# Scores of a unit and head: one matmul with 128 queries on tiles of 64 rows and 128 columns, in place of two with 64 queries on quarter tiles

## Chip, core and metric

The kernel runs on one core of a Trainium2 chip. The metric is the device time of one execution in microseconds (us); before the change the median of three runs is 1308.91 us. The engines are called as the profile calls them: PE (TensorE matmul), PEld (its weight loads, which lie beside the matmuls), DVE (VectorE), ACT (ScalarE), POOL (GpSimd) and SP (the engine that issues most DMAs).

## The reference

Attention over 8 batches of 8 heads, with 576 rows of 64 numbers each, in which only scores close to the row's maximum count, then a feed-forward layer with a squared ReLU on the 4608 x 512 result.

```python
scores = scale * np.matmul(q, k.transpose(0, 1, 3, 2))
thresh = np.max(scores, axis=-1, keepdims=True) - tau
scores = np.where(scores >= thresh, scores, -1000000000.0)
scores = scores - np.max(scores, axis=-1, keepdims=True)
attn = np.exp(scores)
attn = attn / (np.sum(attn, axis=-1, keepdims=True) + 1e-09)
return np.matmul(attn, v).astype(np.float32)
# (B,H,S,D) -> (B*S, H*D), then
h = np.maximum(x @ w_in, 0.0)          # 512 -> 2048
return (h * h @ w_out).astype(np.float32)
```

All matmuls are in float32. The trace shows each of them as two MATMUL records with a LDWEIGHTS each, called its two passes here.

## The kernel before

**Two stages.** The attention fills the first 512 us; the feed-forward layer (lines L825 and L960, each a product of 2 x 2 blocks with seven multiplications, nested twice) fills the rest and is not touched.

**Units.** Heads are taken in pairs, 32 in all: the 64 numbers of the first head lie on partitions 0 to 63, those of the second on 64 to 127. A pair's 576 queries are four units of 128 rows and a rest of 64; the rests of two pairs make one joint unit. So there are 144 units, 128 full and 16 joint. Keys stand as 512 (main) and 64 (rest).

**Periods.** The work is written out by hand, period by period, two units A and B to a period. In period p the scores of A = 2p and B = 2p + 1 are made, the weights of the pair of units before are masked, and the values of the pair before that are summed. Two lists give the order in which a period's steps are issued. CONVERTING is used for the first half of the attention, while POOL, DVE and ACT also convert the feed-forward weights from float64; PLAIN for the rest:

```python
PLAIN = """
    SA c3 T topA0 over U eU s1 SB topA1 powA1 leastA topB0 powB0 c1 s2 PV c4 V fetch
    inv powA0 c5 topB1 powB1 eT maskA1 x xm W eV maskA0 leastB c2 c6 eW maskB0
    maskB1
""".split()
CONVERTING = """
    fetch SA U eU T SB topA0 s1 c1 topA1 topB0 c3 V PV leastA over powA0 topB1
    powA1 powB0 c4 eT inv x maskA1 maskA0 W leastB maskB0 c5 eV c2 powB1 c6 eW maskB1 xm
""".split()
```

Every engine works through its own steps in this order and waits on semaphores for the others. The steps, with their lines in the profile:

- SA (L434, PE): A's scores with the 512 main keys, one result for each head (banks 0 and 5 of the PSUM tile `sc`), then the rest keys of A and of B (64 columns each, in banks 1 and 4). SB (L434): B's main scores, banks 2 and 3.
- T (L398, PE): transposes of a later pair's queries (8) or keys (10) into banks 1 and 4; eT (L403 and L411, ACT) takes them to SBUF, where L403 scales the queries. About every ninth period has no T.
- U, V, W (L380, PE): transposes of softmax weights; with W come the row factors (L515, PE), called "ones" below. eU, eV, eW (L523, ACT) take them to SBUF.
- PV (L532, PE): weights times values, into banks 0 and 5; x (L644 on DVE in PLAIN, L642 on ACT in CONVERTING) takes them out.
- topA0, topA1, topB0, topB1 (L452, DVE): copies a unit's scores of one head to SBUF and reduces each row. pow (L462, ACT): the exponential. mask (L467, DVE): threshold and row sum. Small steps: least (L459, POOL), over (L474, POOL), inv (L477, DVE). s1 and s2 (L122 and L125, POOL): sums of feed-forward weights.

**Tiles of the array.** The profile prints the part of the array that a matmul uses, rows by columns: `64*64` is a quarter tile, `64*128` half of the rows with all columns. Scores, ones and PV use `64*64`, the transposes T, U, V, W `64*128`. The two heads lie on different rows. A score matmul of a full unit has half of its queries, c = 0 or 1, as weights and puts them on one half of the columns, so that a unit's main scores are four matmuls on the four quarters.

**Where the halves come from.** A transpose takes 64 rows at a time. The two halves r of the queries go to two PSUM banks, and `then` in `turn` takes each half, 256 columns for four units, to its own half of `qT`.

Of the kernel before, what the change touches and what calls it, by code (L numbers as in the profile page):

```python
# [48 lines left out]
def kernel(  # L49
# [25 lines left out]
    nc = tc.nc  # L75
    B, H, S, D = q.shape
    P = 128
# [3 lines left out]
    FULL = S // P  # L81
# [190 lines left out]
    loaded, loaded_v, turned, weights = {}, {}, {}, {}  # L272
    CH = NB + FULL
    HALF = P // 2
# [57 lines left out]
    def places(i):  # L332
        if i not in turned:
            turned[i] = (
                sb.tile([P, MAIN], FP32, tag="qT", bufs=Q_RING, name="qT"),
                sb.tile([P, S], FP32, tag="kT", bufs=K_RING, name="kT"),
                sb.tile([P, REST], FP32, tag="qR", bufs=K_RING, name="qR"),
            )
        return turned[i]
# [3 lines left out]
    def ask_ahead(i, which):  # L343

        while asked[which] < min(len(pairs) - 1, i + (2 if i else 1)):
            asked[which] += 1
            (load_k if which else load_q)(asked[which])
# [7 lines left out]
    def touch(what, made, at, size, key=0):  # L355

        if at is None:
            return
        on = range(at // BANK, (at + size - 1) // BANK + 1)
        met = {made.ins.engine}  # L360
        for kind, other, others, its in reversed(touched):
            e = other.ins.engine
            if e == made.ins.engine:
                continue
            if on[-1] < others[0] or others[-1] < on[0]:
                if any({what, kind} == {x, y} and any((key - its) % n == 0 for n in rings) for x, y, rings in MEET):
                    continue
                tc.declare_no_dep(made.ins, other.ins, reason="other banks")
            elif e not in met:
                met.add(e)  # L370
                tc.add_manual_dep(made.ins, other.ins.name, behind, reason="same bank")
        touched.append((what, made, on, key))
        while len(touched) > 300:
            touched.popleft()
# [12 lines left out]
    def joined(to):  # L387

        return to.rearrange("p (t r q) -> p r t q", r=2, q=HALF)

    def turn(i, which, spots, other=None):

        nat, to = loaded.pop((i, which)), places(i)
        of = [nat[:, t, :] for t in range(FULL)] + ([loaded.pop((i, 2))] if which else [])
        for t, x in enumerate(of):
            for r, (spot, at) in enumerate(spots):
                rows = ds(r * HALF, HALF)
                made = nc.tensor.transpose(spot[:, ts(t, HALF)], x[rows, :], ident[rows, rows])  # L398
                touch("turns", made, at, BANK)
        half = FULL * HALF  # L400

        def scaled(to, spot):
            touch("turned", nc.scalar.activation(out=to, in_=spot[0], func=AF.Identity, scale=qscale[:, :]), spot[1], BANK, i)  # L403

        def then():
            part = lambda r, x, n: (spots[r][0][:, ds(x, n)], spots[r][1])
            if which:
                for r, n in ((0, half), (1, half + REST)):
                    spot = part(r, 0, n)
                    copy_by = other if r and other else nc.scalar.copy  # L410
                    touch("turned", copy_by(to[1][:, ds(r * half, n)], spot[0]), spot[1], BANK, i)  # L411
                scaled(to[2], part(0, half, REST))
                ask_ahead(i, 1)
            else:
                for r in range(2):
                    scaled(to[0][:, ds(r * half, half)], part(r, 0, half))
                ask_ahead(i, 0)

        return then
# [3 lines left out]
    def scores(n, rest):  # L423

        of, t = units[n]
        at_k, count = (MAIN, REST) if rest else (0, MAIN)
        for j in range(2):
            first = n % 2 != j
            to = (3 * j + 1) * BANK + first * (BANK - REST) if rest else (3 * j + 2 * first) * BANK
            for c in range(2):  # L430
                rows, at = ds(j * D, D), ds(c * HALF, HALF)
                qT, kT, qR = turned[of[c]]
                lhs = qT[rows, ds((c * FULL + t) * HALF, HALF)] if t < FULL else qR[rows, :]
                made = nc.tensor.matmul(  # L434
                    sc[at, ds(to, count)], lhs, kT[rows, ds(at_k, count)], start=True, stop=True
                )
                touch("scores", made, to, count, of[c])
# [170 lines left out]
    def period(p):  # L608
# [51 lines left out]
        def scored_a():  # L660
            if has(A):
                scores(A, False)
                scores(A, True)
                scores(B_, True)
                softmax(A)
# [336 lines left out]
    with tc.manual_schedule():  # L1002
        with ExitStack() as stack:
            sc = stack.enter_context(tc.tile_pool(name="sc", bufs=1, space=PSUM)).tile([P, 6 * BANK], FP32, name="sc")
# [219 lines left out]
```

## Time and profile before

| | |
|---|---|
| time, three runs | 1307.8, 1308.91, 1309.66 us (median 1308.91) |
| profiled execution | 1308.12 us, of which its span 1306.3 us |
| busy in the span | PE 1284.5 us (98%), PEld 1159.8, DVE 1010.8 (77%), ACT 845.7, POOL 916.4 |
| L434 matmuls (scores) | 2304 records, the first at 7.6 us, the last at 498.9 us |
| granted TensorE clock | 0.998 of full speed |

The 1.8 us between span and time lie outside the profiled instructions. Matmul records overlap: a matmul's recorded duration holds its way through the array, so the distance from the start of one group to the start of the next is what a group costs PE, and that is how the rows of the timeline are read here. "x16" counts records, two for each matmul.

### The profile page before, as it was taken

Reading aid. Unit: us, or ns where it says so; the run is one execution under the profiler, and the core shown is the slowest. Engines: PE = TensorE matmul, PEld = TensorE weight load, DVE = VectorE, ACT = ScalarE, POOL = GpSimd, SP = SyncE. Lnnn points to the kernel's source line nnn. Section 1 sums busy time; section 2 is a strip of 40 time slices with the busy share of each in tenths; the row PEclk is TensorE's granted clock in tenths of the full one; section 3 lists DMA queues with packets and bytes.
Section 4 is the critical chain, followed back from the end, with each engine's and each line's share of the span. In section 5 each row is a group of like instructions: output and inputs, shape, how many; then the busy total and the mean of one; then the engine's idle time right before and its main releaser. Section 6 shows DMA issues by size and latency. Waiting matters only on the chain.

```text
span 1306.3 us, 47872 instructions
## 1 busy us (share of the span) xinstructions
PE 1284.5 (98%) x19483; PEld 1159.8 (89%) x19483; DVE 1010.8 (77%) x2431; ACT 845.7 (65%) x1498; POOL 916.4 (70%) x1023
## 2 busy tenths in 40 slices
PE   8999999999999999999999999999999999999998
PEld 5777777677777777999999999999999999999998
DVE  5999999999999996877787778777646654665463
ACT  5999999888898985657665766675523432433240
POOL 2777778755555320978897789768777777777775
PEclk9999999999999999999999999999999999999999
DMA  6565666544333313466556665569645234522511
GB/s 153 145 160 140 169 182 188 147 103 104 89 78 79 79 41 80 133 200 218 182 181 194 203 208 164 180 247 393 245 158 162 63 105 158 162 68 96 162 34 33
DMA packets 247035, 192.12 MB, mean 147 GB/s; under 512 B 97184, under 2 KB 195488, under 8 KB 246816
## 3 DMA queue, kind: packets, MB, share of 16 engines
q1 hardware_dynamic: 245504, 188.66, 48.5%
q8 instruction: 153, 2.51, 0.8%
q14 instruction: 66, 0.54, 0.2%
q10 hardware_dynamic: 1312, 0.41, 0.1%
HBM read 116.65 MB, written 72.35 MB: 145 GB/s over the span
## 4 chain that ended last, share of the span: by engine, by line
PE 87%; ACT 5%; DMA 3%; DVE 3%; issue 1%; POOL 1%; SPq 0%; ACTq 0%; DVEq 0%; POOLq 0%
PE po L960 29%; PE ph L825 28%; PE sc L532 11%; PE sc L434 10%; PE pt L380 5%; DVE arena L452 3%; ACT arena L462 2%; PE sc L515 2%; DMA wall<-w 2%; PE sc L398 2%; ACT arena L523 1%; PE sc L380 1%; DMA g<-arena 1%; ACT arena L403 0%; ACT c L771 0%
## 5 line engine op out<-in xcount | busy, mean ns | idle before, releaser
L125 POOL TENSOR_TENSOR arena<-arena 128x512 f32<-128x512 f32 (+1 forms) x314 | 378.1, 1223 | 129.1 <-DVE arena L125 115.1
L960 PE MATMUL po<-wall,arena 128*128 128x128 f32 x3528 | 394.7, 275 | 1.4 <-ACT arena L737 1.4
L960 PEld LDWEIGHTS po<-wall,arena 128*128 128x128 f32 x3528 | 394.3, 192 | 1.8 <-ACT arena L737 1.8
L825 PE MATMUL ph<-arena,wall 128*128 128x128 f32 x3528 | 394.2, 275 | 0.7 <-DVE arena L644 0.7
L825 PEld LDWEIGHTS ph<-arena,wall 128*128 128x128 f32 x3528 | 394.0, 192 | 0.8 <-issue 0.8
L125 DVE TENSOR_TENSOR arena<-ph,arena 128x512 f32<-128x512 f32 x378 | 256.3, 688 | 86.3 <-PE ph L825 63.2
L122 POOL TENSOR_TENSOR arena<-arena 128x128 f32<-128x128 f32 (+2 forms) x314 | 255.4, 814 | 53.8 <-DMA arena<-w 37.6
L125 DVE TENSOR_TENSOR arena<-po,arena 128x128 f32<-128x128 f32 x378 | 108.4, 290 | 168.6 <-PE po L960 164.5
L467 DVE SCALAR_TENSOR_TENSOR arena<-arena 128x576 f32<-128x576 f32 x288 | 237.4, 860 | 1.3 <-POOL arena L459 0.8
L452 DVE TENSOR_SCALAR_CACHE_REDUCE arena<-sc 128x576 f32<-128x576 f32 x288 | 205.0, 747 | 14.6 <-ACT arena L523 4.8
L462 ACT ACTIVATE arena<-arena 128x576 f32<-128x576 f32 x288 | 208.1, 773 | 11.8 <-DVE arena L452 8.5
L771 ACT COPY c<-arena 128x512 f32<-128x512 f32 (+1 forms) x303 | 173.5, 579 | 49.6 <-DVE arena L122 41.7
L532 PEld LDWEIGHTS sc<-arena 64*64 64x64 f32 x5760 | 159.2, 133 | 36.7 <-DVE arena L452 20.2
L532 PE MATMUL sc<-arena 64*64 64x128 f32 (+1 forms) x5760 | 180.8, 262 | 2.7 <-DVE arena L452 1.3
L434 PE MATMUL sc<-arena 64*64 64x64 f32 (+1 forms) x2304 | 176.9, 414 | 6.2 <-ACT arena L403 4.2
L122 DVE TENSOR_TENSOR arena<-arena,c 128x512 f32<-128x512 f32 (+1 forms) x267 | 174.9, 663 | 5.5 <-ACT c L771 4.0
L523 ACT COPY arena<-pt 128x1024 f32<-128x1024 f32 x144 | 146.4, 1017 | 30.5 <-PE pt L380 29.4
L737 ACT COPY arena<-po 128x128 f32<-128x128 f32 x63 | 16.6, 264 | 186.7 <-PE po L960 184.0
L380 PEld LDWEIGHTS pt<-ident,arena 64*128 64x128 f32 x2304 | 83.4, 139 | 39.4 <-ACT arena L523 30.1
L737 ACT COPY arena<-ph 128x512 f32<-128x512 f32 x63 | 36.6, 581 | 123.1 <-PE ph L825 122.5
L434 PEld LDWEIGHTS sc<-arena 64*64 64x64 f32 x2304 | 74.3, 134 | 45.1 <-ACT arena L403 15.1
L380 PE MATMUL pt<-ident,arena 64*128 64x64 f32 x2304 | 102.2, 228 | 2.3 <-ACT arena L523 2.3
(50 smaller groups left out, 922.2 us busy)
## 6 DMA issues: line engine op xcount, KB each, us to landing
g<-arena SPq DMA_DIRECT2D x144, 256.0 KB, 2.6
arena<-g SPq DMA_DIRECT2D x144, 256.0 KB, 4.6
w<-arena SPq DMA_DIRECT2D x60, 256.0 KB, 2.4
wall<-w SPq DMA_DIRECT2D x49, 256.0 KB, 5.2
arena<-w SPq DMA_DIRECT2D x44, 256.0 KB, 3.3
arena<-in_v_dram SPq DMA_DIRECT2D x32, 288.0 KB, 4.0
out_dram<-arena SPq DMA_DIRECT2D x70, 128.0 KB, 2.2
arena<-in_q_dram SPq DMA_DIRECT2D x64, 128.0 KB, 4.0
```

The lines of the kernel that those rows point to most:

```text
L122: e.tensor_tensor(out=out, in0=x, in1=y, op=ALU.subtract)
L125: e.tensor_tensor(out=out, in0=x, in1=y, op=ALU.add)
L380: made = nc.tensor.transpose(pt[:, r, ts(slot, HALF)], of[rows, :], ident[rows, rows])
L434: made = nc.tensor.matmul(sc[at, ds(to, count)], lhs, kT[rows, ds(at_k, count)], start=True, stop=True)
L452: made = nc.vector.tensor_scalar(out=s[:, j, :], in0=sc[:, ds(at, S)], scalar1=1.0, scalar2=None, op0=ALU.mult, op1=ALU.min, accum_out=nmx ...
L462: nc.scalar.activation(out=w[:, :, j, :], in_=of(j), func=AF.Exp, bias=nmx[:, j : j + 1], scale=-1.0)
L467: nc.vector.scalar_tensor_tensor(out=w[:, :, j, :], in0=of(j), scalar=thr[:, j : j + 1], in1=w[:, :, j, :], op0=ALU.is_le, op1=ALU.mult, a ...
L523: touch("weights", nc.scalar.copy(joined(to), whole(pt, 0, count)), at, 2 * BANK, m)
L532: made = nc.tensor.matmul(sc[ds(u * D, D), ds(5 * j * BANK + row, count)], loaded_v[i][rows, (c - (u != j)) % CH, :], wT[m][rows, ds(weigh ...
L771: nc.scalar.copy(c, y)
L825: nc.tensor.matmul(to[:, j, :], W_IN[m, k][:, ts(j, P)], of[k][:, m - 1, :], start=(not more and j == 0), stop=True, skip_group_check=True,)
L960: nc.tensor.matmul(to, g[:, j, :], w[:, j, :], start=(not more and j == 0), stop=(j == 3), skip_group_check=True)
```

## The change

For full units the score matmuls of the two halves become one, with 128 queries as weights on a tile of 64 rows and 128 columns. So that the 128 queries of a unit lie side by side, the two scaled copies of L403 now write stretches of 64 columns at a distance of 128 (unit, half, query) where each wrote 256 columns in a row (half, unit, query). Joint units keep the four quarter tiles, as their halves belong to different pairs. The order of all steps is the same. On PE, 512 of the 1152 score matmuls fall away.

```diff
             else:
                 for r in range(2):
-                    scaled(to[0][:, ds(r * half, half)], part(r, 0, half))
+                    spot, at = part(r, 0, half)
+                    scaled(joined(to[0])[:, r, :, :], (spot.rearrange("p (t q) -> p t q", q=HALF), at))
                 ask_ahead(i, 0)
@@ scores
+            rows = ds(j * D, D)
+            if t < FULL:
+                qT, kT, _ = turned[of[0]]
+                made = nc.tensor.matmul(
+                    sc[:, ds(to, count)], qT[rows, ts(t, P)], kT[rows, ds(at_k, count)], start=True, stop=True
+                )
+                touch("scores", made, to, count, of[0])
+                continue
             for c in range(2):
-                rows, at = ds(j * D, D), ds(c * HALF, HALF)
+                at = ds(c * HALF, HALF)
                 qT, kT, qR = turned[of[c]]
-                lhs = qT[rows, ds((c * FULL + t) * HALF, HALF)] if t < FULL else qR[rows, :]
+                lhs = qR[rows, :]
                 made = nc.tensor.matmul(
                     sc[at, ds(to, count)], lhs, kT[rows, ds(at_k, count)], start=True, stop=True
                 )
```

## The prediction

> **What bounds the kernel now.** I read the busy time by stretch first, then PE's timeline in a period of each list, then DVE's, then the waits and the chain that ended last. Only the attention (first 512 us) is touched. Its two halves differ:
>
> ```profile
> core 0: us, PE busy (x) PEld busy (x) DVE busy (x) ACT busy (x) POOL busy (x), PEclk, DMA share, GB/s
> 36.75:250.40 213.65, 209.50 (x5188) 156.89 (x5181) 212.66 (x571) 205.03 (x368) 171.15 (x211) 1.00 0.62 162
> 265.50:483.60 218.10, 215.34 (x5662) 162.43 (x5666) 209.79 (x629) 194.38 (x305) 109.59 (x153) 1.00 0.36 83
> ```
>
> In the first stretch (CONVERTING) DVE is free for 1.0 us of 213.65: it is the bound there. In the second (PLAIN) DVE is free for 8.3 us, and PE's starts follow each other without a hole. One plain period on PE, start and duration of each group:
>
> ```profile
> 311.84 0.46 PE L515 MATMUL sc<-ident,arena 64*64 64x64 f32 x16
> 312.12 1.27 PE L434 MATMUL sc<-arena 64*64 64x512 f32 x24
> 313.32 0.53 PE L398 MATMUL sc<-ident,arena 64*128 64x64 f32 x10
> 313.69 0.66 PE L380 MATMUL pt<-ident,arena 64*128 64x64 f32 x16
> 314.28 1.09 PE L434 MATMUL sc<-arena 64*64 64x512 f32 x8
> 315.19 2.47 PE L532 MATMUL sc<-arena 64*64 64x128 f32 x72
> 317.58 0.71 PE L380 MATMUL pt<-ident,arena 64*128 64x64 f32 x16
> 318.13 0.29 PE L380 MATMUL sc<-ident,arena 64*128 64x64 f32 x4
> 318.35 0.46 PE L515 MATMUL sc<-ident,arena 64*64 64x64 f32 x16
> ```
>
> From ones to ones this is 6.51 us (6.44 where T has 8 records, 6.35 where there is no T). DVE in the same period:
>
> ```profile
> 313.96 0.76 DVE L452 TENSOR_SCALAR_CACHE_REDUCE arena<-sc 128x576 f32<-128x576 f32 x1
> 314.65 0.75 DVE L452 TENSOR_SCALAR_CACHE_REDUCE arena<-sc 128x576 f32<-128x576 f32 x1
> 315.33 0.08 DVE L452 DVE_READ_ACCUMULATOR arena<-sc 128x1 f32 x1
> 315.48 0.76 DVE L452 TENSOR_SCALAR_CACHE_REDUCE arena<-sc 128x576 f32<-128x576 f32 x1
> ```
>
> In every plain period with a T, topA0 starts 0.33 to 0.35 us after T's last matmul starts (here 313.62 and 313.96): T writes banks 1 and 4, which the tops read. topB0 (315.48) starts 0.70 after SB's last (314.78), in all. PE in turn starts part of PV, then waits for topA1:
>
> ```profile
> PEld sc L532 <- DVE arena L452: 10.1, 34, 0.5
> ```
>
> So a plain period is one loop: topA1 ends, PV goes on, V, W, ones, SA, T, then topA0 and topA1 again. U, SB and PV's start run beside the two tops, with a wait of some 0.2 to 0.3 us at PV. **Only what changes between the start of SA and the end of T counts**; a gain at SB goes into that wait. A second loop lies just below: PV's end, x, three masks, topA0. It sets the periods without T, 6.35 us, and is the floor for the others.
>
> **Prices on PE**, from group starts. A slot (one pass on each of two row halves, 64 moving columns, tile 64*128) takes 0.062 us; four quarter tiles 0.058. A pass of 512 columns takes 0.43. Where the tile shape changes, the last slot lasts 0.09 longer and the next group's first slot 0.05 longer. Check: U with 16 records is 8 slots, 0.50; in the plain period it takes 0.59 (313.69 to 314.28; it leaves to another shape), in a converting one 0.55 (208.40 to 208.94; it enters from one).
>
> **The change, part by part.**
>
> 1. *In front of SA.* The ones use 64*64 and SA, new, 64*128: a change where none was. Ones to SA goes from 0.28 to 0.28 + 0.11 = 0.39, and SA's first pass gets the 0.05. Added: 0.16.
> 2. *SA itself.* Main: two passes of 0.43 each as before, since the two heads' tiles run side by side as four quarters did. Rest keys of A and B: four slots of 0.062 for four of 0.058. Added: 0.02.
> 3. *SA to T.* No shape change any more: 0.09 less at SA's end and 0.05 less in T, and 0.02 less as two tiles start in place of four. Removed: 0.16.
>
> Start of ones to start of T's last matmul: before 0.28 + 1.20 + 0.30 = 1.78, after 0.39 + 0.91 + 0.25 + 0.25 = 1.80. **A plain period costs 0.01 to 0.02 us more**; with 21 regular ones, +0.2 us.
>
> 4. *U, SB and PV's start.* U loses 0.09, SB starts warm (0.05 less), and then SB to PV becomes a change (+0.11, and 0.05 in PV). U to PV: 1.50 before, 1.47 after; SB's results come 0.15 earlier. topB0 then follows topA1 at once, its DVE gap here (0.07) vanishes, and x still waits for PV's end. Worth 0 on the loop. If this cover went, the later start of PV would cost 0.05 a period.
> 5. *Joint units.* A joint unit keeps quarter tiles. Where it is B, the sequence is ones, SA (64*128), A's rest, B's rest (64*64), T: two more changes, 0.14 each: +0.29. Three plain periods: +0.9 us. Where it is A, one change stands among the rests in place of one behind them: 0.
> 6. *SA's late start.* Four plain periods have SA waiting on ACT:
>
> ```profile
> 285.73 1.09 PE sc L434 x24
> 287.88 1.02 ACT arena L523
> 289.71 2.01 ACT arena L462 x3
> 292.60 1.32 PE sc L434 x24
> ```
>
> The chain that ended last runs there through the exponentials and L403's two copies; the first of the three exponentials follows topB0's end, and topB0 follows SB. Here SB's 0.15 counts (visible DVE idle before topB0 is 0.13): four times, -0.6 us.
>
> 7. *Copies of L403.* Same elements, in stretches of 64. Their row now is 0.46 us (256 columns); the nearest rows in stretches, L523, take 0.60 for 512 and 1.02 for 1024, no more for each element. 0; bounds -0.05 to +0.05 each, 16 pairs of copies, hidden but in the four periods above.
> 8. *CONVERTING.* PE saves about 0.3 us a period: two shape changes fewer (SA, U, T, SB and V are now alike). But PV there waits for topA1 already, 0.3 us or so a period, and DVE has no gap. 33 periods, worth 0; bound 1.0 us, DVE's free time. A joint B costs 0.29 and finds that wait as cover.
> 9. *Waits.* The instruction order on DVE shows one difference: topB0 drops a wait on ACT, for an eW that ended long before (313.82 against 315.48). 0. DMA issues and POOL stay as they are.
>
> Sum: 0.2 + 0.9 - 0.6 = +0.5 us on 1308.12, the profiled execution (span 1306.3 and 1.8 around it), so 1308.6. The median of the runs is 0.8 above that execution, so against it **1309.4 us**. A measurement of this kernel can tell about 0.2% (2.6 us) from no change; this forecast is no change.
>
> **One rule weighed.** In the transposes, two passes on the same row half with 128-column weights start 0.062 us apart, hardly above their streaming, so the second load lies under the first pass. Against it stands the Trainium skill, "TensorE: Matmul & The Clock Gate", Part 3 (What overlaps and what doesn't): a weight load overlaps a running matmul only where the row group differs. By it, second passes of SA and SB, now on two row groups only, would wait for their loads. The same page's section on LDWEIGHTS has the time grow with columns, about 107 ns for 128 columns against 53 for 64, an estimate from its formula; by that alone the entry into SA costs 0.05 more in 24 plain periods and the sum is 1310.6. The records here say 139 ns for 128 columns and 133 for 64, and the first slot after a change is 0.05 longer for both.
>
> **Rivals.**
>
> - *Slower: SA's wide weights are not hidden.* No row shows 512 moving columns on a 64*128 tile. If SA's second pass waits for its load, the dearest price is the load's record, 0.14 us, in front of T, in 24 plain periods: +3.4, so 1312.8. With the entry dearer by half of that as well it is 1314.5. From 0.09 us a period it counts as slower. This is also what the rule above would do. Against: the 0.062 us slots; and passes of 128 columns on the full array (L960) come 0.11 apart.
> - *Slower by much: the two heads' tiles don't run side by side at 512 columns.* Then every SA and SB has 0.86 more, over 72 periods at least 60 us: 1370. Against: transposes of the two row halves start together in every slot.
> - *Faster: T's gate opens.* If the switch in front of SA is partly hidden (0.11 or more of the 0.16), T ends before DVE wants it, and the x loop takes over: 0.09 to 0.16 a period in 21, so -2.6; with -0.6 from part 6 and +0.5 left of part 5 it gives 1306.2, just past the mark. Against: each of the changes from 64*64 with 64 columns to 64*128 shows the same 0.15 from last start to first, so no cover is seen.
> - *Faster: CONVERTING is not bound by DVE.* One mask there takes 1.13 us where others take 0.74, always under POOL's 2.04 us of L212. If that stretch followed PE's pace, up to 0.3 in 33 periods: 1299. Against: L212 follows DVE's own tops.
> - *The change doesn't do what it says.* The instruction order shows the wide matmuls in place; only joint units keep quarters. No chance of its own.
>
> **How the numbers follow.** Forecast 0.52 (1307 to 1311). Wide weights not hidden 0.26, tiles one after the other 0.02. T's gate opens 0.17, CONVERTING freed 0.03. Each unknown price stays inside its case. Slower by over 0.2%: 0.26 + 0.02 and 0.02 of the forecast's upper tail = 0.30. Faster: 0.17 + 0.03 = 0.20. Within: 0.50. The range reaches from 1304.5 (the opened gate, with the 1.0 us bound of part 8 and 0.7 for topB0 starting earlier than priced in part 6) to 1314.5, the upper end of the first rival, and leaves out 0.05 and the tails; the forecast's own range is 1307 to 1311.
>
> **What would show it.** SA, T, U, SB and V all on 64*128 without a gap; ones to SA 0.39; SA's two passes 0.48 and 0.43 apart; plain periods of 6.52 and 6.46; one plain period in nine 0.29 longer; PV's wait for topA1 still there, no DVE idle before topB0; CONVERTING periods at 7.08 as before, with longer PV waits. It is wrong if SA's second pass starts later than 0.48, if T's last matmul moves by more than 0.05, or if converting periods change at all.

## The result, and the profile after

The changed kernel takes 1311.83 us (median of 12 runs), the kernel before 1308.45 us (12 runs beside it). The ratio is 1.0029, 95% interval 1.0021 to 1.0036: slower by 3.4 us. The forecast was 1309.4, no change, with a range of its own of 1307 to 1311. The time lies above that, in the part of the whole range (1304.5 to 1314.5) that stood for the first rival.

The busy time by stretch, the stretches being those of the prediction:

```profile
core 0: us, PE busy (x) PEld busy (x) DVE busy (x) ACT busy (x) POOL busy (x), PEclk, DMA share, GB/s
36.75:250.40 213.65, 212.44 (x4778) 157.25 (x4778) 213.65 (x575) 204.52 (x372) 171.17 (x211) 1.00 0.61 164
265.50:483.60 218.10, 217.32 (x5081) 164.32 (x5079) 206.75 (x617) 189.27 (x299) 108.60 (x151) 1.00 0.35 82
```

In the first stretch DVE has no free time at all any more; PE has 410 records less than before and is busy 2.9 us longer. In the second DVE has more free time than before (11.4 us for 8.3), PE less (0.8 for 2.8), and fewer instructions of DVE, ACT and POOL fit into it. This points at PLAIN, and at PE. To see how much is lost where, here is the same view cut at a period's start near 265 us and at the start of the last attention period, first of the kernel before, then of the changed one:

```profile
0.00:265.53 265.53, 254.04 (x6013) 188.79 (x6013) 250.45 (x674) 241.97 (x433) 191.45 (x244) 0.99 0.61 160
265.53:496.57 231.04, 228.02 (x6011) 171.79 (x6015) 222.34 (x667) 205.03 (x319) 112.08 (x159) 1.00 0.35 81
496.57:1306.30 809.73, 802.40 (x7473) 799.17 (x7464) 538.03 (x1092) 398.67 (x748) 612.84 (x620) 1.00 0.50 162
```

```profile
0.00:264.31 264.31, 256.49 (x5501) 190.45 (x5501) 249.60 (x674) 239.65 (x433) 189.86 (x244) 0.99 0.60 160
264.31:499.71 235.40, 234.62 (x5507) 178.17 (x5507) 223.60 (x667) 203.54 (x319) 112.11 (x159) 1.00 0.34 79
499.71:1309.60 809.89, 802.37 (x7458) 799.40 (x7452) 537.68 (x1092) 398.67 (x748) 613.05 (x620) 1.00 0.49 162
```

The counts of DVE, ACT and POOL agree in each row, so these are the same periods. The second number is the length: -1.22 us before PLAIN, +4.36 in PLAIN, +0.16 behind. In PLAIN PE has 504 records less and is busy 6.6 us longer.

One plain period on PE, the one shown in the prediction:

```profile
311.34 0.44 PE L524 MATMUL sc<-ident,arena 64*64 64x64 f32 x13
311.71 1.52 PE L434 MATMUL sc<-arena 64*128 64x512 f32 x12
313.06 0.48 PE L398 MATMUL sc<-ident,arena 64*128 64x64 f32 x10
313.37 0.66 PE L380 MATMUL pt<-ident,arena 64*128 64x64 f32 x16
313.87 1.08 PE L434 MATMUL sc<-arena 64*128 64x512 f32 x4
314.88 2.46 PE L541 MATMUL sc<-arena 64*64 64x128 f32 x72
317.27 0.72 PE L380 MATMUL pt<-ident,arena 64*128 64x64 f32 x16
317.83 0.29 PE L380 MATMUL sc<-ident,arena 64*128 64x64 f32 x4
318.05 0.46 PE L524 MATMUL sc<-ident,arena 64*64 64x64 f32 x16
```

(Lines: ones L524, wide scores L434, scores of joint units L443, PV L541, tops L461; the first row's group began ahead of the window.) SA has 12 records for 24, and yet SA to T is 1.35 us, where it was 1.20. From SA to the next SA (318.44) the period is 6.73, where the kernel before has 6.51 to 6.52. The tops of the same period, on DVE:

```profile
313.27 0.08 DVE L476 DVE_READ_ACCUMULATOR arena<-arena 128x1 f32 x1
313.65 0.76 DVE L461 TENSOR_SCALAR_CACHE_REDUCE arena<-sc 128x576 f32<-128x576 f32 x1 [0.30 <-issue]
...
314.34 0.75 DVE L461 TENSOR_SCALAR_CACHE_REDUCE arena<-sc 128x576 f32<-128x576 f32 x1
...
315.02 0.75 DVE L461 TENSOR_SCALAR_CACHE_REDUCE arena<-sc 128x576 f32<-128x576 f32 x1
```

DVE is done with the masks and stands for 0.30 us ahead of topA0 (0.09 in the kernel before); topB0 (315.02) follows topA1 at once. DVE now waits for T, and PE for topA1:

```profile
PEld sc L541 <- DVE arena L461: 25.4, 36, 0.8
```

This row of the waits covers 265 to 500 us (total, times, longest); the kernel before has 12.5 us in 40 waits there. The loop of the prediction holds, then, and it got longer between ones and T. The prediction had taken the load of 128 columns from the transposes. The loads of the new matmuls have rows of their own now. Groups of instructions in that window, weight loads of the kernel before first, then the wide score loads and the rest-key matmuls of the changed kernel:

```profile
L380 PEld LDWEIGHTS pt<-ident,arena 64*128 64x128 f32 x1136 | 40.9, 139 | 7.1 <-issue 4.6 <-ACT arena L523 1.5
...
L434 PEld LDWEIGHTS sc<-arena 64*64 64x64 f32 x1152 | 31.5, 133 | 25.2 <-ACT arena L403 11.3 <-issue 7.7 <-DVE arena L644 1.0
```

```profile
L434 PEld LDWEIGHTS sc<-arena 64*128 64x128 f32 x504 | 39.3, 187 | 16.6 <-issue 9.9 <-ACT arena L403 4.2
...
L434 PE MATMUL sc<-arena 64*128 64x64 f32 x252 | 18.6, 260 | 0.0
```

The number behind the busy time is the mean of one, in ns. With 128 columns a transpose's load takes 139 ns, a score's 187, against 133 with 64 columns. And a rest-key matmul takes 260 ns, where it took 218.

Single records of the trace show where that goes, as starts of PE's passes in the changed kernel and in the kernel before (same period):

- last start of ones to SA's first pass: 0.149, was 0.038. This is the change of tile shape, priced 0.11, and it is 0.11.
- SA's first pass to its second: 0.533, was 0.431. Priced 0.48. The first pass's record is 0.69 us long where a pass with its weights in place has 0.59.
- second pass to the first rest slot: 0.43 in both.
- first rest slot to T's first pass: 0.39, was 0.34. The slots' records begin 0.056, 0.112 and 0.112 apart, T's 0.111 behind the last. Before, 0.058 each and 0.149 to T. Priced 0.25. The records of slots two to four are 0.272 long where the first's is 0.216: they begin 0.056 before they stream, and hold that wait.
- T's first to last: 0.26, was 0.31, as priced.

The weight loads of the changed kernel in this stretch:

```profile
311.71 0.30 PEld L434 LDWEIGHTS sc<-arena 64*128 64x128 f32 x4
312.24 0.19 PEld L434 LDWEIGHTS sc<-arena 64*128 64x128 f32 x2 [0.24 <-issue]
312.67 0.42 PEld L434 LDWEIGHTS sc<-arena 64*128 64x128 f32 x6 [0.23 <-issue]
312.95 0.20 PEld L398 LDWEIGHTS sc<-ident,arena 64*128 64x128 f32 x2
```

Each pass has one load on each of the two row halves. The first rest slot's starts with SA's second pass (312.24) and lies under it. The second slot's starts with the first slot (312.67), the next two 0.11 and 0.22 later: here the loads follow each other, and the slots wait for them.

Sum: +0.11 + 0.10 + 0.05 - 0.05 = +0.21 in front of the tops, and +0.21 is what the period gained.

### The profile page after: what moved, and what is told of

Read it like the earlier page. It is cut to its first block, busy times and chain, and to the rows that moved or that the text cites. A ratio compares the mean times of both kernels' runs of the same rounds, so it can differ in the third digit from the quotient of the medians.

```text
span 1309.6 us, 45824 instructions
## 1 busy us (share of the span) xinstructions
PE 1293.5 (99%) x18459; PEld 1168.0 (89%) x18459; DVE 1010.9 (77%) x2431; ACT 841.9 (64%) x1498; POOL 915.0 (70%) x1023
## 4 chain that ended last, share of the span: by engine, by line
PE 89%; ACT 4%; DMA 3%; DVE 2%; issue 1%; POOL 0%; SPq 0%; DVEq 0%; ACTq 0%; POOLq 0%
PE po L969 29%; PE ph L834 28%; PE sc L541 12%; PE sc L434 10%; PE pt L380 5%; DMA wall<-w 2%; ACT arena L471 2%; PE sc L524 2%; PE sc L443 1%; PE sc L398 1%; DVE arena L461 1%; ACT arena L532 1%; PE sc L380 1%; DMA g<-arena 1%; DVE arena L476 0%
## 5 line engine op out<-in xcount | busy, mean ns | idle before, releaser
L461 DVE TENSOR_SCALAR_CACHE_REDUCE arena<-sc 128x576 f32<-128x576 f32 x288 | 203.0, 747 | 15.3 <-ACT arena L532 6.4
L471 ACT ACTIVATE arena<-arena 128x576 f32<-128x576 f32 x288 | 205.2, 772 | 7.5 <-DVE arena L461 7.0
L541 PEld LDWEIGHTS sc<-arena 64*64 64x64 f32 x5760 | 157.2, 133 | 39.8 <-DVE arena L461 32.5
L541 PE MATMUL sc<-arena 64*64 64x128 f32 (+1 forms) x5760 | 181.6, 263 | 1.3 <-DVE arena L461 0.2
L434 PE MATMUL sc<-arena 64*128 64x64 f32 (+1 forms) x1024 | 171.5, 449 | 3.6 <-ACT arena L403 2.6
L380 PEld LDWEIGHTS pt<-ident,arena 64*128 64x128 f32 x2304 | 86.3, 141 | 34.2 <-ACT arena L532 27.5
L434 PEld LDWEIGHTS sc<-arena 64*128 64x128 f32 x1024 | 80.9, 189 | 39.9 <-issue 25.6
```

The lines of the kernel that those rows point to most:

```text
L380: made = nc.tensor.transpose(pt[:, r, ts(slot, HALF)], of[rows, :], ident[rows, rows])
L434: made = nc.tensor.matmul(sc[:, ds(to, count)], qT[rows, ts(t, P)], kT[rows, ds(at_k, count)], start=True, stop=True)
L461: made = nc.vector.tensor_scalar(out=s[:, j, :], in0=sc[:, ds(at, S)], scalar1=1.0, scalar2=None, op0=ALU.mult, op1=ALU.min, accum_out=nmx ...
L471: nc.scalar.activation(out=w[:, :, j, :], in_=of(j), func=AF.Exp, bias=nmx[:, j : j + 1], scale=-1.0)
L541: made = nc.tensor.matmul(sc[ds(u * D, D), ds(5 * j * BANK + row, count)], loaded_v[i][rows, (c - (u != j)) % CH, :], wT[m][rows, ds(weigh ...
```

## Theories and experiments

**Load theory.** The weights of a wide score matmul take about 0.11 us to load, twice those of a quarter tile. The load is hidden under a 512-column pass, but it shows where nothing or little runs meanwhile: behind a change of tile shape (SA's first pass) and in 64-column slots. **Shape theory.** Only the changes of tile shape cost, and the one in front of SA costs more than priced. **Layout theory.** L403's copies in stretches of 64 columns became slower. And for the rest of the prediction: whether SA to T is all that counts in PLAIN, and DVE all that counts in CONVERTING.

All edits stand against the changed kernel. In all but the first and third, the quarter path reads the joined layout:

```diff
-                lhs = qR[rows, :]
+                lhs = qT[rows, ds(t * P + c * HALF, HALF)] if t < FULL else qR[rows, :]
```

**e1_after_again**, no edit.

> The changed kernel once more, as the mark for the others of this set; 3 us above the kernel before (ratio 1.002 to 1.003). Nothing is told apart by it alone.

Measured: 1311.31 us, kernel before 1308.18; 1.0028 (1.0018 to 1.0038).

**e1_layout.** No wide score matmuls, but the new copies:

```diff
-            if t < FULL:
+            if t < FULL and False:
```

> Only the copies are changed (stretches of 64 columns at a distance of 128); every score matmul is on its quarter tile as before. Load theory (weights of 64 rows and 128 columns take about 0.11 us to load, 0.05 more than quarter tiles, and this shows where what runs meanwhile is short: in front of SA and in the four rest slots): the copies cost nothing, 0 +- 0.7 us against the kernel before, plain periods 6.51. Layout theory (the copies in stretches are what became slower): their row rises above 0.46 us and the loss of 3 us is here already.

Measured: 1307.36 us, 0.9992 (0.9983 to 1.0002). Regular plain periods 6.51. L403's row, 256 columns:

```profile
L403 ACT ACTIVATE arena<-sc,qscale 128x256 f32<-128x256 f32 x28 | 11.4, 455 | 0.0
```

455 ns, the 0.46 us of the kernel before. The layout theory falls: without the wide matmuls no loss is seen.

**e1_rest128_wide.** The changed kernel; in PLAIN the rest-key passes of full units read the 64 keys twice over:

```diff
+            keys = turned[of[0]][1][rows, ds(at_k, count)]
+            span = count
+            if rest and t < FULL and not converts(n // 2):
+                span = 2 * count
+                to -= first * count
+                keys = bass.AP(tensor=keys.tensor, offset=keys.offset, ap=[keys.ap[0], [0, 2], keys.ap[1]])
...
-                    sc[:, ds(to, count)], qT[rows, ts(t, P)], kT[rows, ds(at_k, count)], start=True, stop=True
+                    (sc[:, ds(to, span)].rearrange("p (a b) -> p a b", b=count) if span > count else sc[:, ds(to, span)]), qT[rows, ts(t, P)], keys, start=True, stop=True
```

("..." stands for lines left out.)

> The changed kernel, but in the plain stretch the rest-key matmuls of full units move 128 columns (the 64 rest keys twice, the second copy to columns that nobody reads), so a pass streams twice as long under the same weights. Load theory: a rest slot is already 0.112 us long because its weights take that long, and streaming 128 columns takes 0.107, so it is hidden: 0 to +0.5 us against the changed kernel, rest slots still 0.11. Stream theory (the slot got longer for a reason that adds to the streaming, such as a drain between wide tiles): slots of 0.16, 0.05 x 4 in some 21 periods in front of T: +4 us against the changed kernel.

Measured: 1314.16 us (5 runs), 1.0048 (1.0035 to 1.0061), 2.8 us above the changed kernel's 1311.31 beside it. In the trace:

```profile
310.95 1.57 PE L440 MATMUL sc<-arena 64*128 64x512 f32 x12
312.36 0.47 PE L398 MATMUL sc<-ident,arena 64*128 64x64 f32 x10
312.66 0.67 PE L380 MATMUL pt<-ident,arena 64*128 64x64 f32 x16
```

SA to T is 1.41 for 1.35. The single records: slots 0.109, 0.112, 0.112 apart and T 0.111 behind the last. Here no slot's record is longer than the first's by more than 0.003. Without the 0.056 of waiting that the records of slots two to four hold in the changed kernel, its slots stream 0.111, 0.112 and 0.112 apart, and T follows the last by 0.056. So twice the streaming leaves the steps from slot to slot as they were: load and streaming run side by side and do not add, and the stream theory (slots of 0.16) falls. Its +4 us lay nearer to the measured +2.8 than the load theory's 0 to +0.5 all the same. The expectation had overlooked the last slot, which streams in the open ahead of T (0.111 for 0.056): +0.05 in each period with a T, and PLAIN is 1.6 us longer than in the changed kernel's run beside it (237.04 for 235.43). The other 1.2 us of the medians lie within their intervals.

**e1_rest128_narrow.** The same edit on e1_layout's quarter tiles.

> The layout kernel, on quarter tiles, but in the plain stretch the rest-key matmuls of full units move 128 columns. Load theory: here a slot is bound by streaming, 0.058 before, about 0.11 now, so 0.05 x 4 in front of T in each plain period with a T: periods of about 6.7, +4 to +5 us against the kernel before, much the same as the changed kernel. If T's end is not what sets the period (rival: PV's loop sets it), 0 to +1 us.

Measured: 1312.44 us, 1.0034 (1.0020 to 1.0047).

```profile
312.64 0.46 PE L530 MATMUL sc<-ident,arena 64*64 64x64 f32 x16
312.93 1.48 PE L449 MATMUL sc<-arena 64*64 64x512 f32 x24
314.33 0.53 PE L398 MATMUL sc<-ident,arena 64*128 64x64 f32 x10
```

SA to T is 1.40 for 1.20, the period 6.71: 0.20 put between SA and T, by streaming in place of loads, is 0.20 in the period. That is the prediction's loop, shown without any wide tile.

**e2_rest_wide**, **e2_sa_main_wide**, **e2_sb_wide.** One part of the change each:

```diff
-            if t < FULL:
+            if t < FULL and rest:                      # e2_rest_wide
+            if t < FULL and n % 2 == 0 and not rest:   # e2_sa_main_wide
+            if t < FULL and n % 2 == 1 and not rest:   # e2_sb_wide
```

> Only the rest-key scores of full units are wide (64 rows, 128 columns); main scores stay on quarter tiles. The number of tile-shape changes in front of T is that of the kernel before, one (main to rest, in place of rest to T). Load theory: the first rest slot shows its whole load behind the change (0.16 long), the next three take 0.112 each, T's first load is shown no more (-0.05): about +0.20 in each plain period with a T, 6.71, so +4 to +5 us against the kernel before, much as the changed kernel. Shape theory (only the changes cost, 0.14 each): as many as before, 0 to +0.5 us, periods of 6.51 to 6.53.

> Only SA's main scores are wide; rest keys and SB stay on quarter tiles. Three changes in front of T (ones to SA, main to rest, rest to T) for one. Load theory: +0.11 for the change in front of SA, +0.10 for the load it shows, +0.14 for main to rest: +0.35 in each plain period with a T, 6.86, +7 to +9 us against the kernel before. Shape theory: two changes of 0.14 to 0.16 more, +0.30, +6 to +7 us. The first pass of SA tells the two apart: its second pass starts 0.53 (load) or 0.48 (shape) after it.

> Only SB is wide. In the plain stretch nothing changes between the start of SA and the end of T; U to SB loses a change, SB to PV gets one. If start of SA to end of T is all that counts: regular plain periods 6.51 as before, the four periods in which SA waits for ACT 0.12 to 0.15 shorter, in sum -0.6 us (0 to -1.0) against the kernel before. If PE's work counts wherever it stands, 0: a change less and a change more.

Measured, the kernel before at 1307.58 us: e2_rest_wide 1313.10 us, 1.0045 (1.0032 to 1.0057); e2_sa_main_wide 1316.66 us, 1.0070 (1.0056 to 1.0083); e2_sb_wide 1306.03 us, 0.9989 (0.9980 to 0.9998). PE in a regular plain period, the first kernel, then the second:

```profile
312.22 0.46 PE L524 MATMUL sc<-ident,arena 64*64 64x64 f32 x16
312.50 1.04 PE L443 MATMUL sc<-arena 64*64 64x512 f32 x8
313.47 0.66 PE L434 MATMUL sc<-arena 64*128 64x64 f32 x8
313.97 0.48 PE L398 MATMUL sc<-ident,arena 64*128 64x64 f32 x10
```

```profile
309.74 0.46 PE L524 MATMUL sc<-ident,arena 64*64 64x64 f32 x16
310.13 1.13 PE L434 MATMUL sc<-arena 64*128 64x512 f32 x4
311.19 0.46 PE L443 MATMUL sc<-arena 64*64 64x64 f32 x16
311.59 0.52 PE L398 MATMUL sc<-ident,arena 64*128 64x64 f32 x10
```

e2_rest_wide has one change of shape in front of T, as the kernel before, and still loses 0.22 in a period (6.73; expected 6.71 by the load theory, 6.51 to 6.53 by the shape theory). The shape theory falls here. In e2_sa_main_wide SA's main part takes 1.06 (310.13 to 311.19) for 0.86, SA's second pass starts 0.53 behind the first, and the period is 6.87, where the load theory has 6.86 and the shape theory some 6.81. Both agree with the load theory within 0.02.

e2_sb_wide is the part that gained (-0.6 us was expected, the medians give -1.55). Its regular plain periods are 6.51 to 6.52; the periods with SA's late start fall from 7.04 to 6.82. The ends of such a period, the kernel before and e2_sb_wide:

```profile
350.92 0.46 PE L515 MATMUL sc<-ident,arena 64*64 64x64 f32 x16
351.82 0.66 PE L434 MATMUL sc<-arena 64*64 64x512 f32 x4 [0.44 <-ACT arena L403]
```

```profile
349.68 0.46 PE L524 MATMUL sc<-ident,arena 64*64 64x64 f32 x16
350.33 0.66 PE L443 MATMUL sc<-arena 64*64 64x512 f32 x4 [0.19 <-ACT arena L403]
```

PE's wait for L403's copy is 0.44 before and 0.19 here; ahead of it topB0 starts 1.60 behind topA0 in the kernel before and 1.36 here. SB's earlier end reaches SA by way of topB0, the exponentials and the copies, as the prediction's part 6 has it. That is 0.9 us for four periods; the interval of the medians allows 0.3 to 2.6.

**e2_T_quarter.** Scores as in e1_layout; in PLAIN, T on quarter tiles, so that the change of shape stands behind T:

```diff
-                made = nc.tensor.transpose(spot[:, ts(t, HALF)], x[rows, :], ident[rows, rows])
...
+                for col, n in parts:
+                    cols = ds(col, n)
+                    spun = spot[cols, ts(t, HALF)]
+                    if n < P:
+                        made = nc.tensor.matmul(spun, x[rows, cols], ident[rows, rows], start=True, stop=True)
+                    else:
+                        made = nc.tensor.transpose(spun, x[rows, cols], ident[rows, rows])
```

(In PLAIN `parts` is the two halves of the columns, in CONVERTING all of them.)

> All scores on quarter tiles, and in the plain stretch T too: its 64 rows by 128 columns become two matmuls with the identity on 64 by 64 each, so that ones, SA, rests and T have one shape, and the change stands behind T, in front of U. If T's end sets the period: T ends 0.14 earlier (0.09 and 0.05), the loop over PV, x and the masks takes over 0.09 to 0.16 below, and U's later start lies under PV's wait for topA1: -0.09 to -0.14 in some 24 periods, -2.2 to -3.4 us against the kernel before. If instead PV's start sets it, 0 or +0.1 in each period, up to +3 us.

Measured: 1312.88 us, 1.0038 (1.0026 to 1.0051); slower, where -2.2 to -3.4 us was expected. The reason is in one row:

```profile
313.39 0.76 PE L402 MATMUL sc<-ident,arena 64*64 64x64 f32 x40
```

A transpose has one record; the same step as a matmul with the identity has two, like every float32 matmul here. Ten transposes became twenty matmuls and forty records, ten slots in place of five. The change of shape did go (last rest slot to T 0.04 for 0.15), but T's first to last took 0.55 for 0.31, so T ended 0.13 later, and the period is 6.63: +0.12. So the period follows T's end upwards again. The expectation's rival, PV's start, gives about +0.1 as well, but no more than +3 us in all, where the medians give +5.3 (3.4 to 6.7). For T speaks also that topA0 still starts 0.33 behind T's last matmul, and PV's main part 0.82 behind the start of topA1 (0.81 before). Whether the period would follow an earlier T downwards was not seen.

**e3_conv_wide**, **e3_best.**

```diff
-            if t < FULL:
+            if t < FULL and converts(n // 2):                                       # e3_conv_wide
+            if t < FULL and (converts(n // 2) or (n % 2 == 1 and not rest)):        # e3_best
```

> All scores of full units are wide in the converting stretch, none in the plain one. If DVE sets the converting periods: 7.06 to 7.08 as before, with longer waits of PE at PV, 0 to -1.0 us against the kernel before. If PE's work counts there: two shape changes less in a period, up to 0.3 in 33 periods, down to -9 us. The load theory adds nothing here: what a load shows on PE lies under the same wait.

> Wide scores in the converting stretch and for SB in the plain one; SA's main and rest keys stay on quarter tiles in the plain stretch. The start of SA to the end of T is that of the kernel before: plain periods 6.51, the four in which SA waits for ACT 6.82 for 7.04: -0.9 us from these, and 0 to -1.0 from the converting stretch; 1306.0 to 1308.0 where the kernel before has 1308.0, the fastest of the kernels here. If PE's work counted wherever it stands, the converting stretch would give up to -9 us.

Measured, the kernel before at 1308.22 us: e3_conv_wide 1307.46 us, 0.9997 (0.9988 to 1.0005); e3_best 1305.37 us, 0.9980 (0.9970 to 0.9990). Nine converting periods, after which the pattern repeats, take 63.55 us with wide scores and 63.65 to 63.75 without (single longer periods left aside): some 0.6 us in 33 periods is all. That alone does not show that DVE sets these periods, for PE's way did not get shorter. From the start of ones to the start of PV a converting period takes 4.21 us where T has ten transposes, for 4.22 before, and 4.21 where it has eight, for 4.16: what the changes of shape give back, the loads take. It does show that T's end is no gate here: T's last matmul starts 2.50 us behind the start of ones for 2.41 before, and the period is no longer for it.

e3_best is the fastest here: 2.9 us below the kernel before (1.3 to 3.9). Its trace accounts for about half: 0.9 in the four late periods, 0.6 in CONVERTING. For the rest no period can be named; it lies within the interval.

The parts side by side, in a regular plain period with ten transposes:

| scores on wide tiles | period, us | time against before |
|---|---|---|
| none (e1_layout) | 6.51 | 0.9992 |
| SB | 6.52 | 0.9989 |
| rest keys | 6.73 | 1.0045 |
| SA's main | 6.87 | 1.0070 |
| all (the change) | 6.73 | 1.0029 |

## Why the prediction was right or wrong

**The forecast.** The time lies within the whole range because that range was stretched for a rival; the case that was forecast, no change, did not come. Two of the prediction's own signs of being wrong did: SA's second pass starts 0.53 behind the first, where 0.48 was the limit, and T's last matmul moved by 0.21, where 0.05 was. Converting periods changed too, if only by 0.01 to 0.02.

**The two stretches and the loop: right for PLAIN as far as tested.** PLAIN follows the way from ones to T upwards at 1:1 (e1_rest128_narrow +0.20 for +0.20, e2_T_quarter +0.12 for +0.13), and a gain at SB is worth nothing in a regular period (e2_sb_wide). That DVE sets CONVERTING rests on its busy time, which fills the stretch; no run put it to the test.

**Parts 1 to 3: the term that was mis-sized.** Start of ones to start of T's last matmul was to go from 1.78 to 1.80; it went to 2.00. The change in front of SA was priced right (0.11). The first slot behind it was priced 0.05 longer, and is 0.10 longer. The four rest slots were priced 0.062 each, and together with T's entry that should have given back 0.14; it gave back nothing. Both errors have one source: the price of a slot on a 64*128 tile was read from the transposes, "a slot (one pass on each of two row halves, 64 moving columns, tile 64*128) takes 0.062 us". The transposes were the only row with that tile, but not the nearest in kind. The page of the kernel before has, among the costliest groups, a wide load that is no transpose, the feed-forward's, with a mean of 192 ns:

```profile
L960 PEld LDWEIGHTS po<-wall,arena 128*128 128x128 f32 x3528 | 394.3, 192 | 1.8 <-ACT arena L737 1.8
```

The prediction set 139 against 133 ns and concluded that the width costs nothing. The score loads' 187 ns are with this row. The prediction used L960 only as a reason against its rival, because its passes of 128 columns come 0.11 apart. PV's passes of as many columns, with 64-column weights, are 0.109 apart: 128 moving columns take about as long as a wide load, so that row could not speak against the rival.

**The rule weighed.** The Trainium skill, "TensorE: Matmul & The Clock Gate", section on LDWEIGHTS, has the time of a load grow with the columns: by its formula, an estimate, about 107 ns for 128 and 53 for 64. The wide scores agree with it: rest slots 0.112 apart, records 54 ns longer than with 64 columns, 0.10 shown at SA's entry where 0.05 was priced. The transposes do not: 128 columns, 0.062 apart. The prediction let the transposes decide and followed the rule only in one sentence, for SA's entry alone. The same page of the Trainium skill, Part 3, has a load overlap a running matmul only where the row group differs. The trace does not bear that out: a rest slot follows SA's second pass, on the same rows, by 0.43, the time of streaming alone, and its load began with that pass. The kernel before had shown as much: SA's second pass follows the first by 0.43 there, on the same rows. With it falls the place that rival 1 gave the cost, SA's second pass.

**The rivals.** "SA's wide weights are not hidden" came nearest in kind: 128-column loads do show. That it gave +3.4 in 24 periods and the medians show +3.4 is chance: it priced one wait of 0.14 at SA's second pass, which has none. What shows is the load of SA's first pass and those of the rest slots. "T's gate opens" would have needed T to end earlier. It ends later, and DVE's wait ahead of topA0 grew. The two heads' tiles do run side by side at 512 columns (their passes start 0.007 apart), and the wide matmuls are in place. "CONVERTING is not bound by DVE" was not decided, as PE's way there did not shorten.

**Part 4.** SB's passes are 0.485 apart, where 0.43 was expected: its first load shows by 0.05 here too, behind a 64-column slot instead of a change. So PV does not start 0.03 earlier but at the same time (1.51 after U's start; was 1.50). It costs nothing, since PV waits longer for topA1 than before. The cover was named rightly.

**Part 5.** Priced +0.29 for a period with a joint B and 0 with a joint A; measured from SA to SA +0.40 (6.45 to 6.85) and +0.21 (6.56 to 6.77; half of it is the change ahead of the next SA). In their records the same loads show, 0.10 behind a change of shape and 0.05 in a 64-column slot.

**Part 6.** Priced -0.15 in four periods; -0.12 in the changed kernel (7.04 to 6.92), -0.22 where SB alone is wide.

**Parts 7 to 9.** The copies cost nothing that e1_layout could show, and CONVERTING stays within its bound of 1.0 us: right. The reason given for CONVERTING was half wrong: PE was to save 0.3 us a period there and wait longer at PV. It saved nothing up to PV (4.21 for 4.22 and 4.16), and its waits for topA1 in 20 to 250 us are 5.8 us, for 6.4 before. The dropped wait was not looked at by itself.

The sum again: nine plain periods, after which the pattern repeats, gain 1.51 us over e1_layout's, and 3.5 such groups +5.3. The profiled executions show +4.4 in PLAIN, and +5.0 if one period of the kernel before (7.17) is set to the 6.51 of its like. With -0.6 from CONVERTING that makes +4.4 to +4.7, at the upper end of what the medians say (+3.4, interval 2.7 to 4.7); about 1 us is not placed.

## What to carry to other kernels

Price a weight load by a row of the same kind: here transposes with 128 columns went in steps of 0.062 us, float32 matmuls with 128 columns of weights in steps of 0.112. A wider weight tile saves instructions, and pays only where each load lies under a long pass; with short moving operands, or behind a change of tile shape, PE runs at the pace of the loads. Before a change is made everywhere, ask at which place each instance stands: the same edit gained at SB in four periods, took as much as it gave in CONVERTING, and lost in front of the gate of PLAIN.

## What the runs showed of the hardware

- Passes of 64 columns with 128-column float32 weights start 0.112 us apart, and with 128 moving columns still 0.112: load and streaming run side by side, and the longer one counts. With 64-column weights on four quarters they start 0.058 apart.
- At a change of tile shape the next pass starts later, by 0.11 from 64*64 to 64*128 and by 0.09 the other way (last start of U to SB 0.152 for 0.059), and then shows its whole load: 0.10 with 128 columns, 0.05 with 64 or with a transpose's 128.
- Behind a 512-column pass on the same tile shape no load shows (next start 0.43 later), with 64 or 128 columns. A MATMUL record that starts before its weights are in is longer by the wait: 0.693 for 0.589, 0.272 for 0.216.
- A float32 transpose is one pass (one record), the same product by a matmul with the identity two.
